# Starting two token blocks in halves: a new order for the first stage of a scan and two expert layers

## The chip, the cores and the metric

One core of a Trainium2 chip runs the whole program. The metric is the device time of one execution in microseconds (us). Engines are called PE (TensorE), DVE (VectorE), ACT (ScalarE), POOL (GpSimd) and SP (SyncE, which here only issues transfers); each takes its own instructions in the order in which they were written into its queue.

## The reference

Three layers, one after the other, for 3072 tokens of width 256 (4 sequences of 768 tokens, 8 heads of width 32).

```python
# 1. a scan over chunks of each sequence (state N=16 x D=32 for each head)
L = np.exp(cum[:, :, :, None] - cum[:, :, None, :]) * causal
M = np.einsum('bhin,bhjn->bhij', Cc, Bc) * L
y_intra = np.einsum('bhij,bhjd->bhid', M, xc)
y_inter = np.einsum('bhin,bhnd->bhid', Cc, state) * np.exp(cum)[:, :, :, None]
state = decay_full[:, :, None, None] * state + np.sum(Bx, axis=2)
# 2. a dense layer, 256 -> 2048 -> 256
h = x @ w_in
g = np.maximum(0.01 * h, h)
x = g @ w_out
# 3. each token goes to one of 8 experts, 256 -> 1024 -> 256
out[mask] = gate_w[mask, None] * (np.maximum(x[mask] @ w1[e], 0.0) @ w2[e])
```

`cum` is the running sum of log(a) within a chunk. `w_in` and `w_out` arrive as 8-byte floats.

## The kernel before

The 3072 tokens are 24 **chunks** of 128 (six to a sequence) and 6 **blocks** of 512 (four chunks each). A chunk c of the scan passes through named steps: `load` (tiles `ct`, `bt`, `xt`, and for chunks from 4 on `e`), `trmm`, `trc`, `trb`, `trd`, `trde` (transposes on PE and their evictions), `exp` (the decays L into `e`), `cb` and `mul` (the scores and their product with `e`), `bs`, `p3` (PE: output and state update), `st` (DVE: the state), `xa`, `xb` (the output as a high part `xh` by ACT and a rest `xl` by DVE). Each dense product runs as three products of such high and low parts.

The decays of chunks 0 to 3 are made on the chip (`bc`, into PSUM, then `exp`); their causal mask is a POOL instruction after `exp` (L445). For later chunks the running sums go out to DRAM (`cumd`, L364) and come back broadcast to all partitions as `e` (L394); POOL masks them (L399, before `exp`).

A block j of the dense layer has 16 **inner tiles** f of 128 columns. For one inner tile, written here with one number 16j+f: `h` is six matmuls of 512 columns on PE (L655), `sa` on ACT, `gg` on DVE, `gh` on ACT, `gl` on DVE, and `y` is six more matmuls (L695) that add into two PSUM banks which stay open over all 16 inner tiles. The two banks that hold `h` alternate, so `h` of one tile waits until `gg` of the tile two before it is done. `h.0` needs all four chunks of block 0, and from f=4 on each four inner tiles need another piece of the weights.

The weights come in four pieces of 1 MiB for each matrix (`raw.i.k`, `raw.o.k`) through three buffers, and each half piece is converted by two ACT steps (`hb`, `lb`), two DVE instructions (`or`, L605 and L606), one ACT cast and one subtraction on DVE or POOL.

What stands in which order is one long string, `PLAN`. Its tokens are run one by one, and on PE, DVE, ACT, POOL and SP the instructions keep that order. Ahead of it, outside of the string, stand the first loads, the constants (`consts_a`, `consts_b`) and nine matmuls on zeros that keep PE busy (L1107). Within the string, `warm` (L1127) and `wy` (L1133) are more matmuls on zeros. The third layer (`m1`, `m2`) follows when its tokens are sorted, from about 360 us on.

Of the kernel before, what the change touches and what calls it, by code (L numbers as in the profile page):

```python
# [19 lines left out]
NEG = -1.0e30  # L20
# [11 lines left out]
    bc.3.0 mul.1.2 trde.2 trc.2 p3.1 load.5 or.o.0.1 raw.i.2 trb.2 exp.3.0 exp.3.1 cb.2 bs.2 xa.1 st.1 cast.o.0.1
    trmm.3 xb.1 mask.3.0 trb.3 mul.2.1 cast.o.0.0 mask.3.1 mul.2.2 trc.3 subg.o.0.0 mul.2.3 mul.2.0 subv.o.0.1 wy.5.1
    p3.2 load.6 hb.i.1.0 cd.3 bs.3 cd.4 lb.i.1.0 cb.3 st.2 xa.2 or.i.1.0 trd.3 wy.3.2 hb.i.1.1 trde.3 lb.i.1.1 mul.3.3
    trmm.4 mul.3.0 trd.4 cast.i.1.0 mul.3.1 xb.2 trde.4 subg.i.1.0 mul.3.2 trb.4 trc.4 wy.3.3 p3.3 load.7 or.i.1.1
    raw.o.2 xa.3 xb.3 cast.i.1.1 st.3 wy.3.4 h.0 subv.i.1.1 mask.4 h.1 sa.0 cd.5 exp.4.0 gg.0 h.2 gh.0 mask.5 sa.1
    exp.4.1 gg.1 gl.0 h.3 gh.1 bs.4 mask.6 hb.o.1.0 y.0 lb.o.1.0 gl.1 hb.o.1.1 or.o.1.0 lb.o.1.1 y.1 sa.2 or.o.1.1
    raw.i.3 sa.3 cb.4 cast.o.1.0 exp.5.1 gg.2 subg.o.1.0 mul.4.1 h.4 mul.4.3 gh.2 mask.7 mul.4.2 hb.i.2.0 gg.3
    lb.i.2.0 mul.4.0 h.5 gl.2 cast.o.1.1 or.i.2.0 gh.3 trmm.5 sa.4 y.2 sa.5 subv.o.1.1 cast.i.2.0 gl.3 hb.i.2.1 trd.5
    p3.4 load.8 gg.4 subg.i.2.0 lb.i.2.1 gg.5 gh.4 y.3 or.i.2.1 raw.o.3 trb.5 hb.o.2.0 lb.o.2.0 h.6 gl.4 gh.5 or.o.2.0  # L40
    trde.5 exp.5.0 h.7 cd.7 st.4 sa.6 y.4 bs.5 sa.7 gl.5 cast.o.2.0 gg.6 xa.4 y.5 subg.o.2.0 gg.7 gh.6 xb.4 cast.i.2.1
    trc.5 exp.6.0 subv.i.2.1 cb.5 gl.6 h.8 hb.o.2.1 mul.5.1 mul.5.3 hb.i.3.0 mul.5.0 lb.o.2.1 y.6 mul.5.2 gh.7
    or.o.2.1 sa.8 h.9 lb.i.3.0 gg.8 cast.o.2.1 or.i.3.0 h.10 gh.8 sa.9 subv.o.2.1 exp.6.1 p3.5 gl.7 hb.i.3.1 gg.9
    trmm.6 load.9 y.7 lb.i.3.1 gl.8 trb.6 cast.i.3.0 or.i.3.1 h.11 sa.10 gh.9 gg.10 subg.i.3.0 cast.i.3.1 y.8 trc.6
    xa.5 subv.i.3.1 sa.11 mask.8 xb.5 hb.o.3.0 h.12 gh.10 gl.9 lb.o.3.0 gg.11 y.9 exp.7.0 bs.6 gl.10 cb.6 or.o.3.0
    exp.7.1 h.13 hb.o.3.1 mul.6.0 mul.6.2 cast.o.3.0 mul.6.1 y.10 mul.6.3 lb.o.3.1 subg.o.3.0 gh.11 p3.6 sa.12 bs.7
    gl.11 sa.13 trmm.7 gg.12 xa.6 load.10 trd.7 trb.7 y.11 trde.7 trc.7 gh.12 xb.6 st.6 exp.8.1 gl.12 h.14 gg.13
    exp.8.0 or.o.3.1 cb.7 sa.14 y.12 mul.7.1 gh.13 mul.7.2 mul.7.0 cast.o.3.1 h.15 mul.7.3 mask.9 gg.14 subv.o.3.1
    gh.14 trmm.8 gl.13 p3.7 sa.15 exp.9.0 gl.14 y.13 load.11 cd.8 gg.15 xa.7 trb.8 trc.8 exp.9.1 trd.8 xb.7 y.14 bs.8
    cd.9 bt trde.8 gh.15 h.16 gl.15 h.17 sa.16 bs.9 st.7 gg.16 cb.8 sa.17 gh.16 y.15 gg.17 mul.8.3 mul.8.2 h.18  # L50
    mul.8.1 evA.0 evV.0 gh.17 mul.8.0 mask.10 h.19 sa.18 gl.16 exp.10.1 lg.0 gg.18 p3.8 sa.19 lt.0 gl.17 exp.10.0
    cd.10 l2.0 load.12 st.8 trmm.9 trd.9 xa.8 h.20 r1.0 trde.9 trb.9 r2.0 rx.0 y.16 sa.20 xb.8 trc.9 gg.19 rp.0 gh.18
    r3.0 yr.0.0 be.0 y.17 yc.0.0 mask.11 gl.18 put.0 yr.0.1 exp.11.1 h.21 gg.20 gh.19 cd.11 bs.10 y.18 yc.0.1 gl.19
    sa.21 ro.0 exp.11.0 gg.21 trmm.10 trd.10 y.19 trc.10 trde.10 gh.20 trb.10 h.22 gl.20 gh.21 gl.21 h.23 sa.22 gg.22
    cb.9 sa.23 y.20 gg.23 mul.9.3 mul.9.2 y.21 mul.9.1 gh.22 mul.9.0 gl.22 p3.9 mask.12 gh.23 trmm.11 st.9 xa.9
    load.13 trd.11 trb.11 h.24 xb.9 trde.11 exp.12.1 trc.11 bs.11 gl.23 cb.10 sa.24 y.22 exp.12.0 mul.10.3 mul.10.1
    mul.10.2 mul.10.0 h.25 gg.24 gh.24 p3.10 sa.25 gl.24 gg.25 y.23 xa.10 load.14 st.10 xb.10 h.26 bs.12 gh.25 gl.25
    cb.11 sa.26 h.27 gg.26 mul.11.2 mul.11.1 y.24 mul.11.3 sa.27 mul.11.0 gg.27 p3.11 gh.26 gl.26 y.25 xa.11 load.15
    xb.11 h.28 gh.27 gl.27 y.26 sa.28 cd.13 gg.28 mask.13 y.27 gh.28 exp.13.1 gl.28 h.29 exp.13.0 h.30 sa.29 bs.13
    gg.29 y.28 sa.30 gh.29 gg.30 h.31 gl.29 gh.30 cd.14 gl.30 y.29 sa.31 mask.14 gg.31 trmm.12 exp.14.1 h.32 trc.12  # L60
    gh.31 y.30 trb.12 gl.31 sa.32 exp.14.0 gg.32 cb.12 y.31 gh.32 mul.12.3 mul.12.2 mul.12.0 mask.15 mul.12.1 h.33
    evA.1 evV.1 gl.32 exp.15.0 lg.1 sa.33 p3.12 lt.1 exp.15.1 gg.33 l2.1 st.12 load.16 trmm.13 r1.1 xa.12 h.34 trb.13
    gh.33 r2.1 rx.1 xb.12 y.32 sa.34 trc.13 r3.1 gg.34 rp.1 gl.33 h.35 gh.34 be.1 trd.13 sa.35 h.36 gl.34 put.1
    trde.13 gg.35 cb.13 bs.14 sa.36 cd.15 y.33 gg.36 mul.13.1 mul.13.0 h.37 mul.13.2 gh.35 mul.13.3 gl.35 p3.13 sa.37
    gg.37 yr.1.1 xa.13 load.17 st.13 y.34 yc.1.1 xb.13 bs.15 yr.1.0 gh.36 h.38 yc.1.0 gl.36 ro.1 y.35 sa.38 gg.38
    trmm.14 gh.37 trd.14 trc.14 h.39 trde.14 gl.37 trb.14 cd.16 mask.16 cb.14 sa.39 y.36 gg.39 exp.16.1 mul.14.2
    mul.14.3 h.40 mul.14.0 gh.38 mul.14.1 exp.16.0 gl.38 p3.14 sa.40 y.37 st.14 xa.14 load.18 xb.14 gg.40 y.38 gh.39
    bs.16 gl.39 trmm.15 gh.40 trd.15 trc.15 h.41 trb.15 gl.40 trde.15 cb.15 sa.41 h.42 gg.41 mask.17 mul.15.3 mul.15.2
    y.39 mul.15.0 sa.42 mul.15.1 exp.17.0 gg.42 p3.15 cd.17 gh.41 exp.17.1 y.40 gl.41 load.19 st.15 xa.15 bs.17 h.43
    gh.42 xb.15 gl.42 h.44 sa.43 gg.43 y.41 sa.44 gg.44 y.42 gh.43 gl.43 h.45 gh.44 gl.44 y.43 mask.18 sa.45 gg.45  # L70
    exp.18.1 h.46 gh.45 h.47 sa.46 gl.45 exp.18.0 gg.46 y.44 sa.47 y.45 gg.47 gh.46 gl.46 trmm.16 gh.47 h.48 trc.16
    trb.16 gl.47 trd.16 sa.48 y.46 mask.19 trde.16 gg.48 cb.16 gh.48 exp.19.1 h.49 mul.16.3 mul.16.1 mul.16.0 exp.19.0
    gl.48 y.47 mul.16.2 sa.49 p3.16 evV.2 evA.2 gg.49 lg.2 xa.16 load.20 st.16 gh.49 xb.16 h.50 lt.2 gl.49 bs.18 l2.2
    sa.50 trmm.17 r1.2 trd.17 trb.17 h.51 trde.17 r2.2 rx.2 trc.17 rp.2 sa.51 r3.2 trmm.18 be.2 y.48 trb.18 trc.18
    put.2 gg.51 cb.17 gg.50 y.49 mul.17.2 gh.50 mul.17.3 mul.17.0 h.52 gh.51 mul.17.1 gl.50 gl.51 p3.17 sa.52 cd.19
    gg.52 yr.2.1 xa.17 load.21 bs.19 y.50 yc.2.1 xb.17 h.53 gh.52 gl.52 cb.18 sa.53 y.51 gg.53 mul.18.2 mul.18.1 h.54
    mul.18.3 gh.53 mul.18.0 mask.20 yr.2.0 sa.54 gl.53 p3.18 yc.2.0 gg.54 exp.20.0 ro.2 trmm.19 load.22 st.18 y.52
    trc.19 cd.20 xa.18 trb.19 xb.18 exp.20.1 h.55 gh.54 bs.20 trd.19 y.53 sa.55 gl.54 trde.19 gg.55 h.56 gh.55 gl.55
    cb.19 sa.56 y.54 gg.56 mul.19.3 mul.19.1 h.57 mul.19.0 gh.56 mul.19.2 gl.56 p3.19 cd.21 sa.57 mask.21 gg.57 h.58
    xa.19 load.23 st.19 exp.21.0 xb.19 y.55 sa.58 exp.21.1 gg.58 y.56 gh.57 bs.21 h.59 gl.57 gh.58 gl.58 h.60 sa.59  # L80
    gg.59 mask.22 y.57 sa.60 gg.60 exp.22.0 y.58 gh.59 h.61 gh.60 gl.59 exp.22.1 gl.60 h.62 sa.61 gg.61 y.59 sa.62
# [1174 lines left out]
```

## Time and profile before

| | |
|---|---|
| median of 3 executions | 515.06 us (513.83 to 516.0) |
| the profiled execution | 515.77 us, of which the span from first to last instruction is 514.1 us |
| busy in the span | PE 495.4 us, DVE 327.0, ACT 288.1, POOL 138.1 |
| granted TensorE clock, mean | 0.993 of full speed |

The profiled execution is 0.7 us above the median. Outside of the span lie 1.7 us. Everything below is counted in the span of the profiled execution, from its first instruction.

### The profile page before, as it was taken

How to read it: one execution, taken by the hardware profiler on the slowest of the kernel's cores; microseconds unless marked ns; L12 is line 12 of the kernel's file. 1: busy time of each engine (PE TensorE's matmuls, PEld its weight loads, DVE VectorE, ACT ScalarE, POOL GpSimd, SP SyncE). 2: the span in 40 equal slices, each digit the busy share in tenths (PEclk: the TensorE clock that was granted, in tenths of full speed). 3: DMA queues.
4: the chain of work that ended last, by engine and by line, in shares of the span. 5: the costliest groups of instructions: out<-in, count | busy, mean ns of one | idle time of the engine just before them, and what ended most of it. 6: DMA issues, size and time to landing. Idle time of an engine off the chain costs nothing.

```text
span 514.1 us, 8931 instructions
## 1 busy us (share of the span) xinstructions
PE 495.4 (96%) x3266; PEld 393.5 (77%) x3266; DVE 327.0 (64%) x719; ACT 288.1 (56%) x626; POOL 138.1 (27%) x137
## 2 busy tenths in 40 slices
PE   7878999999999999999999999999999999999994
...
PEclk8999999999999999999999999999999999999998
DMA  7988863367713550417100661220015954310001
GB/s 153 195 190 210 231 162 68 62 89 26 156 20 63 103 112 7 68 15 169 35 1 2 172 232 52 37 8 0 2 42 115 325 177 166 117 52 32 11 21 68
DMA packets 120151, 48.41 MB, mean 94 GB/s; under 512 B 84066, under 2 KB 113891, under 8 KB 120099
## 3 DMA queue, kind: packets, MB, share of 16 engines
...
q0 software_dynamic: 3072, 6.41, 3.9%
...
## 4 chain that ended last, share of the span: by engine, by line
PE 72%; issue 8%; ACT 6%; DVE 5%; POOL 2%; DMA 2%; SPq 2%; POOLq 1%; ACTq 0%; DVEq 0%
PE y L695 22%; PE h L655 22%; PE hp L1025 10%; PE o L1056 9%; PE cb L512 2%; PE psy L552 2%; POOL out_dram L1086 1%; SPq L392 1%; DVE hb L606 1%; PE psy L547 1%; DMA ct<-in_C_dram 1%; PE xps L1006 1%; PE yr L852 1%; DMA e<-cumd 1%; DVE hb L605 1%
## 5 line engine op out<-in xcount | busy, mean ns | idle before, releaser
L662 ACT ACTIVATE sa<-h 128x512 f32<-128x512 f32 x96 | 56.9, 597 | 72.1 <-PE h L655 68.1
L667 DVE TENSOR_TENSOR gg<-sa,h 128x512 f32<-128x512 f32 x96 | 65.4, 685 | 48.4 <-ACT sa L662 47.2
L677 DVE TENSOR_TENSOR gl<-gg,gh 128x512 fp32r<-128x512 f32 x96 | 71.2, 748 | 15.4 <-ACT gh L672 14.0
L655 PE MATMUL h<-xh,wih 128*128 128x512 f32 x192 | 78.4, 408 | 1.0 <-DVE gg L667 1.0
L695 PE MATMUL y<-gh,woh 128*128 128x512 f32 x192 | 79.2, 412 | 0.0
L655 PE MATMUL h<-xl,wih 128*128 128x512 f32 x192 | 75.1, 391 | 0.9 <-DVE xl L576 0.9
L695 PE MATMUL y<-gl,woh 128*128 128x512 f32 x192 | 75.5, 393 | 0.3 <-DVE gl L677 0.3
L695 PE MATMUL y<-gh,wol 128*128 128x512 f32 x192 | 75.0, 391 | 0.0
L655 PE MATMUL h<-xh,wil 128*128 128x512 f32 x192 | 75.0, 391 | 0.0
L672 ACT CAST gh<-gg 128x512 fp32r<-128x512 f32 x96 | 59.1, 619 | 25.2 <-DVE gg L667 19.9
L1043 DVE SCALAR_TENSOR_TENSOR hl<-hp,hh 128x512 fp32r<-128x512 f32 x48 | 32.9, 689 | 59.0 <-ACT hh L1039 50.8
L1056 PE MATMUL o<-w2s,hh 128*128 128x256 f32 x384 | 70.1, 282 | 0.0
L1025 PE MATMUL hp<-x2h,w1s 128*128 128x512 f32 x192 | 65.8, 395 | 0.4 <-issue 0.3
L1039 ACT ACTIVATE hh<-hp 128x512 fp32r<-128x512 f32 x48 | 28.6, 598 | 61.2 <-PE hp L1025 53.9
L1056 PEld LDWEIGHTS o<-w2s,hh 128*128 128x128 f32 x384 | 61.1, 190 | 2.3 <-issue 0.2
L1056 PE MATMUL o<-w2s,hl 128*128 128x256 f32 x192 | 54.1, 282 | 0.0
L835 POOL DMA_INDIRECT il<-ids,pi x24 | 24.8, 1035 | 105.4 <-DVE base L826 67.9
L417 ACT ACTIVATE e<-e,ncum 128x128 f32<-128x128 f32 x160 | 50.5, 394 | 0.0
L399 POOL TENSOR_SCALAR_AFFINE_SELECT e<-e 128x1024 f32<-128x1024 f32 x20 | 23.9, 1195 | 92.1 <-DMA e<-cumd 68.7
L655 PEld LDWEIGHTS h<-xh,wih 128*128 128x128 f32 x192 | 36.0, 188 | 12.6 <-DVE gg L667 2.9
L695 PEld LDWEIGHTS y<-gh,woh 128*128 128x128 f32 x192 | 36.1, 188 | 11.7 <-issue 4.7
L1025 PEld LDWEIGHTS hp<-x2h,w1s 128*128 128x128 f32 x192 | 36.1, 188 | 8.3 <-issue 0.9
...
## 6 DMA issues: line engine op xcount, KB each, us to landing
...
```

The source lines that it names most:

```text
L417: s.activation(out=e[:, h, :], in_=i, func=AF.Exp, bias=ncum[:, cc, b * H + h:b * H + h + 1])
L655: t_.matmul(h, lhsT=w[:, k, fs], rhs=xx[:, k, :], start=(i == 0), stop=(i == 5))
L662: s.activation(out=d["sa"], in_=d["h"], func=AF.Copy, scale=0.01)
L667: v.tensor_tensor(out=d["gg"], in0=d["sa"], in1=d["h"], op=ALU.max)
L672: s.copy(out=d["gh"], in_=d["gg"])
L677: v.tensor_tensor(out=gl, in0=d["gg"], in1=d["gh"].bitcast(F32), op=ALU.subtract)
L695: t_.matmul(y_t[j][k], lhsT=w[:, f, ds], rhs=gg, start=(f == 0 and i == 0), stop=(f == NF - 1 and i == 2))
L835: w = g.indirect_dma_start(out=il[:], out_offset=IndirectOffsetOnAxis(ap=pi[:, q:q + 1], axis=0), in_=ids[:, c0 + q:c0 + q + 1], in_offset ...
L1025: t_.matmul(d["hp", f], lhsT=d[1][:, k, part, fs], rhs=xx[:, k, :], start=(n == 0), stop=(n == 5))
L1039: s.activation(out=e_h(i, f, "hh"), in_=ex[i]["hp", f], func=AF.Relu)
L1043: v.scalar_tensor_tensor(out=e_h(i, f, "hl"), in0=d["hp", f], scalar=0.0, in1=d["hh", f].bitcast(F32), op0=ALU.max, op1=ALU.subtract)
L1056: t_.matmul(d["o", q], lhsT=d[h, f][:, q * P:(q + 1) * P], rhs=d[2][:, f, part, :], start=(start and n == 0), stop=(f == NF2 - 1 and n == ...
```

## The change

Six things change together.

1. **Halves.** Blocks 0 and 1 run their inner tiles in the order block 0 tiles 0 to 7, block 1 tiles 0 to 7, block 0 tiles 8 to 15, block 1 tiles 8 to 15. After the first half of a block its two PSUM banks are copied to SBUF (`part_a` on ACT, `part_v` on DVE); after its second half two DVE additions put the halves together (`evict_a`, `evict_v`; before, one ACT copy and one DVE copy).
2. **Mask by TensorE.** For chunks 0 to 3 a matmul of an identity with a table of 0 and -1e30 opens each `bc` bank; the POOL masks of these chunks are gone.
3. **Decays from 96 rows.** `a` is loaded as 96 rows of 256 in place of 32 rows of 768; clip and logarithm run on that, and two transposes take the place of six.
4. **Loads in written order.** All loads and constants are tokens of the string now. `load` no longer contains the broadcast of `e`, which is a token of its own (`le`), as is the store of `cumd`.
5. **Fewer matmuls on zeros.** 6 in place of 9 at the start, none in place of 15 by `warm`, 8 in place of 14 by `wy`.
6. **A new order** of the whole string.

```diff
-    decay_a bc.0.0 decay_b cd.1 rows exp.0.0 hb.i.0.0 mask.0.0 bc.0.1 end high lb.i.0.0 cr trmm.0 hb.i.0.1 or.i.0.0
...
+    load.0 kg1 load.1 decay_a load.2 kvb kg2 kvc bc.0.1 raw.i.0 decay_b kg3 kv2 load.3 bc.0.0 exp.0.1 raw.o.0 trmm.0
...
+    HALF = NF // 2
...
-    a_sb = ap_.tile([NB * H, S], F32, tag="as", name="a_sb", bufs=1)
+    a_sb = ap_.tile([96, 2 * P], F32, tag="a96", name="a_sb", bufs=1)
...
+        g.affine_select(out=mkf, in_=mkf, pattern=[[1, P]], compare_op=ALU.is_ge, fill=NEG, base=0, channel_multiplier=-1)
+        v.tensor_copy(id16, ident)
+        v.tensor_copy(mk16, mkf)
...
-        for c in range(NCB):
-            t_.transpose(p0[:, c * BH:(c + 1) * BH], a_sb[:, c * P:(c + 1) * P], ident[:BH, :BH])
-        v.tensor_copy(laT.rearrange("p c r -> p (c r)"), p0[:, 0:NCB * BH])
+        for u in range(2):
+            t_.transpose(p0[:, u * 96:(u + 1) * 96], a_sb[:, u * P:(u + 1) * P], ident[:96, :96])
...
+    def attn_load_e(c):
+        b, cc = divmod(c, NCB)
+        sl = slice(cc * P, (cc + 1) * P)
+        e = ch[c]["e"] = e_tile(c)
+        nc.sync.dma_start(out=e, in_=cumd[b * H:(b + 1) * H, sl].unsqueeze(0).to_broadcast([P, H, P]))
...
+        t_.matmul(bc, lhsT=id16, rhs=mk16.unsqueeze(1).to_broadcast([P, 4, P]), start=True, stop=False)
...
-        if j not in y_t:
+        if (f == 0 and j not in y_t) or (f == HALF and j < 2):
             new_y(j)
+        first = (0, HALF) if j < 2 else (0,)
+        last = (HALF - 1, NF - 1) if j < 2 else (NF - 1,)
...
+    def part_a(j):
+        s.copy(out=yt_tile(j)[:, 0, :], in_=y_t[j][0])
...
     def evict_a(j):
-        s.copy(out=yt_tile(j)[:, 0, :], in_=y_t[j][0])
+        if j < 2:
+            v.tensor_tensor(out=yt_tile(j)[:, 0, :], in0=y_t[j][0], in1=yt_tile(j)[:, 0, :], op=ALU.add)
+        else:
+            s.copy(out=yt_tile(j)[:, 0, :], in_=y_t[j][0])
...
-    for _ in range(9):
+    for _ in range(6):
         t_.matmul(wps, lhsT=wt[:, 0:P], rhs=wt, start=True, stop=True)
```

Two places of the new order matter below. The first is SP's queue behind the constants' loads. Before, from the store of the running sums on (`e_402` and `e_496` are the broadcasts for chunks 4 and 5):

```order
L364 DMA cumd_96<-cumrow_264 32x768
L633 DMA raw_324<-in_moe_w_out_dram 128x4x256
L390 DMA ct_401<-in_C_dram 128x8x16
L391 DMA bt_400<-in_B_dram 128x8x16
L392 DMA xt_399<-in_x_dram 128x8x32
L394 DMA e_402<-cumd_96 128x8x128
L390 DMA ct_495<-in_C_dram 128x8x16
L391 DMA bt_494<-in_B_dram 128x8x16
L392 DMA xt_493<-in_x_dram 128x8x32
L394 DMA e_496<-cumd_96 128x8x128
```

Of the change, the same stretch of SP's queue (`e_400` and `e_514` are the broadcasts for chunks 4 and 5):

```order
L390 DMA cumd_96<-cumrow_277 32x768
L415 DMA ct_376<-in_C_dram 128x8x16
L416 DMA bt_375<-in_B_dram 128x8x16
L417 DMA xt_374<-in_x_dram 128x8x32
L431 DMA e_400<-cumd_96 128x8x128
L663 DMA raw_428<-in_moe_w_out_dram 128x4x256
L415 DMA ct_487<-in_C_dram 128x8x16
L416 DMA bt_486<-in_B_dram 128x8x16
L417 DMA xt_485<-in_x_dram 128x8x32
L431 DMA e_514<-cumd_96 128x8x128
```

The second piece of `w_out` moved from ahead of chunk 4 to behind it; ahead of chunk 5 the same transfers stand as before. The piece of `w_in` that followed `e_496` before now follows chunk 7.

The second place is ACT's queue around the first inner tiles. Before, the `exp` of chunk 4 (`e_402`) stands behind the first `sa` (`xh_152` is `xa` of chunks 2 and 3):

```order
L570 CAST xh_152<-psy_547 128x2x128
L595 ACTIVATE hb_596<-raw_208 128x512
L495 ACTIVATE cdt_599<-ps_523,mask2_106 128x128 x2
L600 ACTIVATE lb_597<-raw_208 128x512
L1148 CAST wih_137<-hb_569 128x512
L492 COPY cdt_612<-ps_604 128x128
L471 COPY btt_616<-ps_604 128x128
L570 CAST xh_152<-psy_623 128x2x128
L1148 CAST wih_137<-hb_596 128x512
L662 ACTIVATE sa_676<-h_658 128x512
L417 ACTIVATE e_402<-e_402,ncum_122 128x128 x4
```

Of the change, ACT's queue from the evictions of chunk 3's transposes on (`xh_156<-psy_525` is `xa` of chunk 2, `xh_156<-psy_590` that of chunk 3):

```order
L525 ACTIVATE cdt_522<-ps_506,mask2_106 128x128 x2
L453 ACTIVATE e_400<-e_400,ncum_125 128x128 x4
L600 CAST xh_156<-psy_525 128x2x128
L453 ACTIVATE e_400<-e_400,ncum_125 128x128 x4
L501 COPY btt_582<-ps_547 128x128
L630 ACTIVATE lb_503<-raw_266 128x512
L1176 CAST woh_146<-hb_472 128x512
L600 CAST xh_156<-psy_590 128x2x128
```

Both halves of chunk 4's `exp` moved ahead of `xa` of chunks 2 and 3, on which `h.0` depends. Of the change again, ACT's queue a few rows on (`xh_171` is `xa` of chunk 4, `sa_713` the first `sa`):

```order
L630 ACTIVATE lb_642<-raw_275 128x512
L453 ACTIVATE e_514<-e_514,ncum_125 128x128 x8
L600 CAST xh_171<-psy_685 128x2x128
L692 ACTIVATE sa_713<-h_628 128x512
L522 COPY cdt_716<-ps_676 128x128
L501 COPY btt_721<-ps_676 128x128
L692 ACTIVATE sa_723<-h_661 128x512
```

The `exp` of chunk 5 moved ahead of the first `sa`, too. On PE, `h.0` is followed by `cb` of chunk 4, `h.1`, the transposes of chunk 5, `p3` of chunk 4, `cb` of chunk 5 and then `h.2`; before, `h.0` to `h.3` and the first two `y` ran ahead of `cb` of chunk 4.

## Rows read from the trace of the kernel before

**Rows 1.** The page: PE's busy tenths in 40 slices, granted clock, DMA share.

```profile
PE   7878999999999999999999999999999999999994
PEclk8999999999999999999999999999999999999998
DMA  7988863367713550417100661220015954310001
```

**Rows 2.** Busy time by stretch: PE, PEld, DVE, ACT, POOL, PEclk, DMA share, GB/s.

```profile
0.00:37.91 37.91, 29.77 (x274) 17.29 (x274) 28.79 (x76) 24.56 (x56) 16.60 (x35) 0.95 0.85 179
39.30:70.50 31.20, 29.34 (x154) 21.25 (x154) 27.31 (x52) 28.09 (x65) 7.68 (x6) 1.00 0.85 219
70.50:130.00 59.50, 59.34 (x440) 44.58 (x439) 50.78 (x120) 44.15 (x115) 13.42 (x11) 1.00 0.52 66
130.00:362.00 232.00, 231.62 (x1452) 179.91 (x1451) 154.43 (x357) 128.13 (x286) 41.23 (x36) 1.00 0.33 69
```

**Rows 3.** Timeline of PE: start, length, line, tiles, count, idle before it.

```profile
1.27 3.87 PE L1107 MATMUL wps<-zer 128*128 128x512 bf16 x9 [1.27 <-DVE zer L1104]
29.68 0.67 PE L539 MATMUL psy<-cdt,st 128*128 128x256 f32 x2 [0.57 <-DVE xl L576]
37.91 0.50 PE L655 MATMUL h<-xh,wih 128*128 128x512 f32 x1
39.31 0.50 PE L655 MATMUL h<-xl,wih 128*128 128x512 f32 x1 [0.89 <-DVE xl L576]
45.79 0.39 PE L695 MATMUL y<-gh,woh 128*128 128x512 f32 x1
...
48.28 0.39 PE L695 MATMUL y<-gh,wol 128*128 128x512 f32 x1
48.60 0.71 PE L512 MATMUL cb<-cm,btt 32*128 32x256 f32 x8
54.50 0.27 PE L477 MATMUL ps<-ident,cd 128*128 128x128 f32 x1
55.80 0.49 PE L695 MATMUL y<-gh,woh 128*128 128x512 f32 x1
```

**Rows 4.** 39.3 to 70.5 us, instructions of L655 (h) alone, then of L695 (y).

```profile
39.30:70.50 31.20, 16.64 (x65) 11.66 (x65) 1.00 0.85 219
...
39.30:70.50 31.20, 11.11 (x42) 7.65 (x42) 1.00 0.85 219
```

**Rows 5.** SP's queue: issues, their length.

```profile
5.05 4.80 SPq L392 DMA_DIRECT2D xt<-in_x_dram  x1
25.15 0.37 SPq L633 DMA_DIRECT2D raw<-in_moe_w_out_dram  x1
30.54 0.53 SPq L394 DMA_DIRECT2D e<-cumd  x1
35.78 0.57 SPq L394 DMA_DIRECT2D e<-cumd  x1
```

**Rows 6.** Stretches of 10 us, as in rows 2.

```profile
20.00:30.00 10.00, 7.72 (x101) 4.81 (x99) 8.34 (x21) 7.98 (x20) 5.28 (x8) 1.00 0.92 233
30.00:40.00 10.00, 6.97 (x77) 3.81 (x76) 9.70 (x24) 4.97 (x12) 3.48 (x3) 1.00 0.82 164
50.00:60.00 10.00, 10.00 (x66) 7.49 (x66) 9.44 (x17) 8.61 (x20) 4.25 (x4) 1.00 0.93 275
```

**Rows 7.** Timeline of POOL, DVE and ACT.

```profile
41.27 1.09 POOL L399 TENSOR_SCALAR_AFFINE_SELECT e<-e 128x1024 f32<-128x1024 f32 x1 [2.90 <-DMA e<-cumd]
43.55 0.69 DVE L667 TENSOR_TENSOR gg<-sa,h 128x512 f32<-128x512 f32 x1 [1.48 <-ACT sa L662]
37.49 0.37 ACT L570 CAST xh<-psy 128x256 fp32r<-128x256 f32 x1 [1.63 <-PE psy L555]
40.76 0.60 ACT L662 ACTIVATE sa<-h 128x512 f32<-128x512 f32 x1 [1.19 <-PE h L655]
41.25 1.27 ACT L417 ACTIVATE e<-e,ncum 128x128 f32<-128x128 f32 x4
```

298 lines of the change are left out of this document (148 added, 150 removed).

## The prediction

> **What bounds the kernel now.** I read the page's slices first: PE is at nine tenths or more in every slice but the first four and the last, and it is at full clock from the second slice on [rows 1]. So PE's own work sets the time once it has begun, and only the first stage can give anything back. The stretches say where that stage ends: from 70.5 us on PE is busy 59.34 of 59.5 us and then 231.62 of 232 us, so nothing is left to gain there unless its work shrinks, and the change takes no matmul away behind that point [rows 2]. From 39.3 to 70.5 us PE is busy 29.34 of 31.2 us, but busy overstates it. PE's timeline shows one matmul of 512 columns every 0.226 us (12 of `y`, the first at 45.79, the last at 48.28, so 11 steps), one `cb` 0.71 us, and `p3` with its transpose 1.3 us (54.50 to 55.80) [rows 3]. In that stretch stand 65 matmuls of `h` and 42 of `y` [rows 4]: 107 times 0.226 is 24.2 us. With `cb` of chunks 4 and 5, `p3` of chunk 4 and a pair of transposes (0.27 us, as the one at 54.50) it is 27.2 us, so 4.0 us of the 31.2 are waits. Ahead of it lies the start: `h.0` begins at 37.91 and stalls for `xl` until 39.31 [rows 3].
>
> What is behind those two numbers? DMA. From the second slice on it is at eight or nine tenths for 60 us [rows 1], 0.92 in the third ten us [rows 6], and SP's queue itself is held up: the load of one `xt` takes 4.80 us to issue [rows 5], because the transfers ahead of it have not drained. What comes late is therefore set by how many bytes stand ahead of it. The broadcast `e` of chunk 5 is issued at 35.78 [rows 5] and the POOL mask that needs it starts at 41.27, after 2.90 us of idling for that transfer [rows 7]: 5.5 us from issue to use.
>
> **The change part by part.** Clip and logarithm on 256 columns in place of 768, two transposes for six, and no POOL mask behind the `exp` of the first chunks shorten the head of the chain. Two chunks' conversions move behind `h.0`. All of that is worth time only up to the next thing that is late. That is `e` of chunk 4. ACT's queue now has the first half of chunk 4's `exp` ahead of `xa` of chunk 2, and ACT takes its queue in order, so behind it wait `xa` of chunks 2 and 3, `xb` on DVE, `p3` of chunk 3 and `h.0`.
>
> When does that `e` come? Before, it was issued at 30.54 [rows 5], so with 5.5 us it was usable at 36.0. In the new order the same transfers stand ahead of it but for one piece of `w_out`, 1.05 MB. At the rate of the stretch in which that piece ran, 233 GB/s, this is 4.5 us; at the fastest and slowest of the rows 3.8 and 6.4 us [rows 6]. So it is usable between 29.6 and 32.2; I take 31.5. ACT is there before: `p3` of chunk 2 ran at 29.68 before [rows 3], and with less ahead of it will not be later. From there: mask 1.1 us to 32.6, half an `exp` 1.27 to 33.9, `xa` 0.37 to 34.2 [rows 7]. Then `xb`, four products by DVE and `p3` of chunk 3 (some 2 and 1.3 us) bring `xa` of chunk 3 to 37.5, where it was before, at 37.49 [rows 7]. The second matmul of `h.0` comes at 39.3, as before. All that was saved at the head is waited away.
>
> The next late thing is `e` of chunk 5. Ahead of it stand the same transfers as before, so it is usable at 41.3. All of chunk 5's `exp` now stands ahead of `xa` of chunk 4 and the first `sa`: mask to 42.4, two halves of 1.27 to 44.9, `xa` to 45.3, `sa` 0.60 to 45.9, `gg` 0.69 to 46.6 [rows 7]. Only then may `h.2` take the first bank; `cb` of chunk 5, queued ahead of it, waits for ACT's evictions behind `sa` and ends at about 47.0. PE meanwhile has `h.0`, `cb` of chunk 4, `h.1`, the transposes and `p3` of chunk 4, from 39.3 to about 44.1, and then waits 2.3 us.
>
> From 47.0 the first half of block 0 needs 14 more inner products (`h.2` to `h.7`, `y.0` to `y.7`): 84 matmuls, 19.0 us; `p3` of chunks 5 to 7, 3.9; two `cb`, 1.4; two pairs of transposes, 0.5. That is 24.8 us, to 71.8. I add 0.7 for small waits, a sixth of the 4.0 found above, because ACT and DVE have half of the conversions left to do by then: 72.5.
>
> The kernel before has at 70.5 us `h.0` to `h.10` and `y.0` to `y.6`, two products more (2.7 us), but lacks the 5.8 us of chunks 5 to 7. It reaches the same amount of work at 73.6. The change is 1.1 us ahead. The new turns between halves cost something: at the end of each half PE goes on with `h` of the other block while ACT and DVE copy the banks, so the cover is some 5 us of matmuls against a copy of about 0.6 us; uncovered, four turns would cost 2.4. The two additions on DVE in place of a copy each on ACT and DVE lie beside PE's work, too. I take 0.5 us. The 24 matmuls on zeros that go, and the eight mask matmuls that come, lie in the stage that waits for DMA and are put at nothing; the first as cover for the clock come up below.
>
> Sum: 515.77 - 1.1 + 0.5 = 515.2 us against the profiled execution, and that was 0.7 above the median of the three runs: **514.5 us**.
>
> **A rule against it.** The kernel before spends 38 matmuls on zeros at the start and shows a mean granted clock of 0.95 up to 37.91 us and 1.00 after that [rows 2]. The nine first ones run at 0.43 us each, which is the lower level, 1.2 GHz, against 0.226 at 2.4 GHz [rows 3]. In the change 14 are left, and PE has almost nothing to do while ACT waits for chunk 4's `e`. The Trainium skill, page "TensorE: Matmul & The Clock Gate", section "HAM oscillation — how this bites in real kernels", tells of a kernel whose PE waited for DMA between bursts of matmuls and began each burst at the halved clock. By that rule `h.0`, `h.1`, `cb` and `p3` would start at 1.2 GHz and the sum would be 516 to 517 instead of 515.2; no stretch of the trace of before shows such a wait ahead of `h`, so it can't settle it.
>
> **The rivals.**
> *The transfers come sooner.* SP is never held up by the order it had before, small transfers run together, and the rate rises. For it: 275 GB/s in one stretch [rows 6]. Against: DMA at 0.92 and 0.93 already [rows 6], with the same packets. Each us by which chunk 5's `e` is sooner is a us of the result. From 2 us on (usable at 39.2) it is faster than the bound; at 4 us, 511.
>
> *The clock falls.* Between `p3` of chunk 2 (by about 30) and `p3` of chunk 3 (about 36) PE has little more than a `cb`, a pair of transposes and four matmuls on zeros, so some 4 us of waiting. At half clock `h.0` and `h.1` take 2.4 us longer (12 times 0.2) and `cb` and `p3` up to 2.0, of which the 2.3 us of waiting absorb half: 1 to 2 us. That alone leaves it within the bound. It decides if the lower level holds beyond 47 us, where PE is the bound again: every 2 us cost 1, so from about 50 us on it is slower; held for 10 us, 519.
>
> *DVE becomes the bound.* From 39.3 to 70.5 DVE is busy 27.31 us and ACT 28.09 of 31.2 [rows 2]. The change packs chunks 5 to 7 into the 25 us from 47 on; 16 `gg` and `gl` at 0.69 us [rows 7] are 11 us of DVE's time there, and with three chunks and four or five conversions I estimate it at 23 to 25 us. If it can't run ahead of PE, 3 to 4 us go: 518. For the other side, half of the conversions are due only later.
>
> **How the numbers follow.** A measurement of this kernel can tell about 0.5%, 2.6 us, from no change. My forecast, a change that does at its head what it says and waits it away at chunks 4 and 5, has a chance of 0.52 and lies within that bound, from 512.5 to 517.5. The sooner transfers have 0.25 (faster, around 511), the clock that stays low 0.14 and DVE 0.09 (both slower, 518 to 519). The range reaches into both sides: 510.3 to 519. Faster 0.25, same 0.52, slower 0.23.
>
> **What would show it.** In the profile after: the `exp` of chunk 4 ends several us of idle time on ACT, released by the mask or by `e`, at about 32.6 us; the first matmul of `h` with `xl` at 39.3 (between 38 and 40); `exp` of chunk 5 at 42.4 and the first `sa` at 45.3; a gap on PE ahead of `cb` of chunk 5 of 2.3 us; the first `h` of block 1 at 72.5; after that PE busy without gaps. I am wrong if `h` begins before 36, if the clock in the stretch from 40 to 50 us is well under 1, or if PE waits for `gg` or `gl` between 47 and 72 us by more than 2 us, or at the turns between the halves by more than 1.

## The result, and the profile after

The changed kernel takes 517.40 us (median of 20 runs, 514.35 to 520.07), the kernel before 514.92 (20 runs beside it): a ratio of 1.0052, interval 1.0033 to 1.0071. It is slower by half a per cent. The time lies inside the range and, by 0.1 us, inside the bounds given for the likeliest case (512.5 to 517.5); but that case had the kernel unchanged, at 514.5, and against the kernel beside it, it is slower.

The first stage by windows of ten us: busy us of each engine with counts, granted TensorE clock (1.00 is 2.4 GHz, 0.50 is 1.2 GHz), DMA's share and rate.

```profile
30.00:40.00 10.00, 5.25 (x35) 2.50 (x33) 5.25 (x13) 5.06 (x15) 2.96 (x3) 0.53 0.94 214
40.00:50.00 10.00, 8.15 (x68) 5.59 (x68) 9.39 (x24) 8.54 (x22) 3.71 (x4) 1.00 0.94 232
70.00:80.00 10.00, 10.00 (x66) 8.03 (x59) 9.37 (x16) 8.24 (x18) 2.85 (x2) 1.00 0.84 208
80.00:90.00 10.00, 9.19 (x40) 7.00 (x38) 9.83 (x17) 8.55 (x21) 4.29 (x3) 1.00 0.08 31
90.00:100.00 10.00, 9.37 (x42) 7.72 (x42) 9.83 (x16) 9.07 (x19) 1.30 (x1) 1.00 0.01 2
```

Two things differ from the windows of before [rows 2, 6]. From 30 to 40 us PE is busy for only 5.25 us of ten, and for most of that time at the lower clock. And from 80 to 100 us PE is idle for 1.44 us, where before it was busy for 59.34 of 59.5 us; DVE stands at 9.83 of 10 there.

ACT in the first stage (start, length, line, what it writes and reads, and in brackets the idle time ahead and what ended it):

```profile
33.08 1.28 ACT L453 ACTIVATE e<-e,ncum 128x128 f32<-128x128 f32 x4 [5.84 <-POOL e L435]
34.27 0.35 ACT L600 CAST xh<-psy 128x256 fp32r<-128x256 f32 x1
38.31 0.37 ACT L600 CAST xh<-psy 128x256 fp32r<-128x256 f32 x1 [1.29 <-PE psy L585]
42.75 2.44 ACT L453 ACTIVATE e<-e,ncum 128x128 f32<-128x128 f32 x8
45.77 0.60 ACT L692 ACTIVATE sa<-h 128x512 f32<-128x512 f32 x1
```

These are `exp` of chunk 4, `xa` of chunks 2 and 3, `exp` of chunk 5 and the first `sa`. ACT stands still for 5.84 us until chunk 4's mask is done; the forecast had these rows at 32.6, 34.2 (the end of a half), 37.5, 42.4 and 45.3. PE's rows that answer to them, and those of the new waits:

```profile
35.81 1.19 PE L569 MATMUL psy<-cdt,st 128*128 128x256 f32 x2 [4.75 <-DVE xl L606]
40.44 0.50 PE L685 MATMUL h<-xl,wih 128*128 128x512 f32 x1 [0.29 <-DVE xl L606]
47.95 0.50 PE L685 MATMUL h<-xh,wih 128*128 128x512 f32 x1 [0.18 <-DVE gg L697]
73.41 0.39 PE L685 MATMUL h<-xh,wih 128*128 128x512 f32 x1
87.26 0.50 PE L727 MATMUL y<-gl,woh 128*128 128x512 f32 x1 [0.81 <-DVE gl L707]
90.70 0.50 PE L685 MATMUL h<-xh,wih 128*128 128x512 f32 x1 [0.63 <-DVE gg L697]
94.91 0.39 PE L685 MATMUL h<-xh,wih 128*128 128x512 f32 x1
```

The second matmul of `h.0` comes at 40.44 (before 39.31 [rows 3]), `h.2` at 47.95, and `h.16`, the first of block 1, at 73.41. Nothing is wrong up to there that would cost 2.5 us. The two waits at 87.26 and 90.70 are new.

A later point shows where this leaves the change. When `y.29` starts, both kernels have exactly the same `h`, `y`, `cb` and `p3` behind them. PE's row there, of the change and of the kernel before:

```profile
149.05 0.50 PE L727 MATMUL y<-gh,woh 128*128 128x512 f32 x1
147.22 0.39 PE L695 MATMUL y<-gh,woh 128*128 128x512 f32 x1
```

The change is 1.83 us late there. DVE just ahead of the two waits and in the first stage, and then POOL:

```profile
37.82 1.65 DVE L636 SCALAR_TENSOR_TENSOR hb<-raw,hb 128x512 int32<-128x512 int32 x1
39.97 0.42 DVE L606 TENSOR_TENSOR xl<-psy,xh 128x256 fp32r<-128x256 f32 x1
79.83 0.69 DVE L635 SCALAR_TENSOR_TENSOR hb<-hb,lb 128x512 int32<-128x512 int32 x1
81.16 0.68 DVE L697 TENSOR_TENSOR gg<-sa,h 128x512 f32<-128x512 f32 x1
82.41 1.81 DVE L635 SCALAR_TENSOR_TENSOR hb<-hb,lb 128x512 int32<-128x512 int32 x1
84.25 1.46 DVE L636 SCALAR_TENSOR_TENSOR hb<-raw,hb 128x512 int32<-128x512 int32 x1
85.63 1.57 DVE L707 TENSOR_TENSOR gl<-gg,gh 128x512 fp32r<-128x512 f32 x1
```

```profile
37.10 1.81 POOL L1178 TENSOR_TENSOR wol<-hb,woh 128x512 fp32r<-128x512 f32 x1 [4.05 <-ACT woh L1176]
82.37 1.30 POOL L1178 TENSOR_TENSOR wol<-hb,woh 128x512 fp32r<-128x512 f32 x1 [6.84 <-ACT woh L1176]
83.61 3.04 POOL L435 TENSOR_SCALAR_AFFINE_SELECT e<-e 128x1024 f32<-128x1024 f32 x2
```

The conversion (`or`, L635 and L636) and `gl` take 0.69 us on DVE when POOL is idle, and 1.46 to 1.81 us from 82.41 to 87.2, while POOL subtracts and masks chunks 10 and 11 (82.37 to 86.65). The `gl` that PE waits for at 87.26 is one of them.

### The profile page after: what moved, and what is told of

It reads as the page before. It is cut to its first block, busy times and chain, and to the rows that moved or that the text cites. A ratio compares the mean times of both kernels' runs of the same rounds, so it can differ in the third digit from the quotient of the medians.

```text
span 514.9 us, 8880 instructions
## 1 busy us (share of the span) xinstructions
PE 494.5 (96%) x3245; PEld 394.6 (77%) x3246; DVE 334.0 (65%) x725; ACT 288.4 (56%) x626; POOL 132.4 (26%) x131
## 4 chain that ended last, share of the span: by engine, by line
PE 80%; issue 7%; DVE 7%; POOL 2%; ACT 2%; DMA 1%; POOLq 0%; SPq 0%; DVEq 0%; ACTq 0%
PE y L727 25%; PE h L685 24%; PE hp L1061 9%; PE o L1092 9%; PE cb L542 3%; PE psy L582 2%; POOL out_dram L1122 2%; DVE e L550 1%; PE psy L577 1%; DVE hb L635 1%; PE yr L888 1%; DVE hb L636 1%; PE xps L1042 1%; DMA e<-cumd 1%; DVE gg L697 1%
## 5 line engine op out<-in xcount | busy, mean ns | idle before, releaser
L707 DVE TENSOR_TENSOR gl<-gg,gh 128x512 fp32r<-128x512 f32 x96 | 68.9, 721 | 14.9 <-ACT gh L702 13.5
L727 PEld LDWEIGHTS y<-gl,woh 128*128 128x128 f32 x192 | 36.1, 188 | 8.4 <-DVE gl L707 2.2
L685 PEld LDWEIGHTS h<-xh,wil 128*128 128x128 f32 x192 | 36.1, 188 | 7.9
```

Source lines behind the costliest of these rows:

```text
L685: t_.matmul(h, lhsT=w[:, k, fs], rhs=xx[:, k, :], start=(i == 0), stop=(i == 5))
L707: v.tensor_tensor(out=gl, in0=d["gg"], in1=d["gh"].bitcast(F32), op=ALU.subtract)
L727: t_.matmul(y_t[j][k], lhsT=w[:, f, ds], rhs=gg, start=(f in first and i == 0), stop=(f in last and i == 2))
```

## The experiments

Theories. *Queue*: the head's gain is waited away on ACT behind `e` of chunks 4 and 5. *Clock*: PE's idling costs the upper clock, and that costs time. *DVE*: what is new is the stretch at 80 to 100 us, where DVE can't keep up, by itself or because POOL holds it up. All edits but three (head_only, halves_only, and in before_few0 the number of zeros at the start) are in the order string; `h.16` and `h.8` (the first of block 0's second half) are read in each run's one trace.

| kernel | median us (runs) | ratio to the kernel before beside it | h.16 | h.8 | between |
|---|---|---|---|---|---|
| the change | 517.40 (20) | 1.0052 (1.0033 to 1.0071) | 73.4 | 94.9 | 21.5 |
| after_again | 517.59 (9) | 1.0043 (1.0028 to 1.0058) | 74.3 | 95.8 | 21.5 |
| zeros | 518.06 (12) | 1.0045 (1.0022 to 1.0069) | 76.2 | 97.7 | 21.5 |
| zeros28 | 516.94 (12) | 1.0052 (1.0031 to 1.0073) | 72.8 | 94.2 | 21.5 |
| q4 | 516.72 (12) | 1.0020 (0.9999 to 1.0041) | 73.4 | 94.9 | 21.5 |
| q45 | 518.94 (6) | 1.0092 (1.0071 to 1.0113) | 78.0 | 99.5 | 21.5 |
| q45b | 514.96 (12) | 1.0003 (0.9983 to 1.0024) | 72.2 | 93.7 | 21.5 |
| subg | 516.87 (7) | 1.0061 (1.0039 to 1.0083) | 73.7 | 95.2 | 21.5 |
| late80 | 514.95 (12) | 1.0006 (0.9987 to 1.0025) | 73.8 | 93.2 | 19.5 |
| q45b_late | 513.37 (12) | 0.9973 (0.9955 to 0.9990) | 71.1 | 90.6 | 19.5 |
| masks_late | 519.69 (12) | 0.9942 (0.9913 to 0.9971), see below | 73.9 | 93.8 | 19.8 |
| bt_late | 518.64 (12) | 0.9940 (0.9910 to 0.9970), see below | 74.3 | 94.8 | 20.6 |
| halves_only | 517.62 (12) | 1.0043 (1.0017 to 1.0068) | 75.9 | 97.4 | 21.5 |
| head_only | 520.57 (6) | 1.0093 (1.0057 to 1.0129) | | | |
| before_few0 | 515.41 (12) | 1.0024 (1.0010 to 1.0037) | | | |

**The clock.** Kernel zeros adds 16 matmuls on zeros, zeros28 adds 30, into PE's wait for chunk 4:

```diff
-p3.2 bs.3 exp.4.0 or.o.0.0 trmm.4 load.6 cb.3 xa.2 st.2 exp.4.1 wy.4.1
+p3.2 wy.6.0 bs.3 exp.4.0 or.o.0.0 trmm.4 load.6 cb.3 xa.2 st.2 exp.4.1 wy.14.1
```

> The changed kernel with 16 more matmuls on zeros on PE: six behind p3 of chunk 2 and ten more (14 in place of 4) behind cb of chunk 3, where PE has nothing else to do. Theory 'clock': the granted clock of 0.53 in 30 to 40 us comes from PE's idling, so it rises to near 1 there, p3 of chunk 3 takes 1.3 us again in place of 2.4, the second matmul of h.0 comes at 39.3 to 39.6 in place of 40.44, and the kernel gains 0.8 to 1.4 us on the change. Rival 'queue': what is late is xa on ACT behind exp of chunk 4, so h.0 stays behind 39.3 whatever the clock and the time moves by less than 0.8 us. If the zeros run at the lower level themselves, the clock can't be had back here and nothing moves.

It did not test the theory: PE still waited 4.12 us after its zeros and fell to the lower clock. In its trace the clock also fell a second time, behind `h.2` (granted 0.84 from 50 to 60 us), and there `h.2` to `h.16` took 26.5 us in place of the change's 25.5. So, with `wy.28.1` in place of `wy.14.1`, and the change itself beside it:

> As zeros, but 28 matmuls on zeros behind cb of chunk 3 in place of 14, so that PE is busy from 29.6 to about 36 us, to just ahead of the moment at which p3 of chunk 3 can run in the change (35.81). Theory 'clock': the granted clock stays at 1.00 from 20 to 50 us, p3 of chunk 3 takes 1.3 us in place of 2.4, and the second matmul of h.0, exp of chunk 5, h.2 and h.16 each come about 1 us sooner behind the mask of chunk 4 than in the change (there 7.4, 9.7, 14.9 and 40.4 us behind its end at 33.05); 0.8 to 1.2 us less than the change beside it. Rival 'queue alone': these distances stay as they are, or h.0 is later because the zeros stand ahead of it.

> The changed kernel itself, beside zeros28 on one chip, since the two differ by an us at most. Every theory expects the distances from the end of the mask of chunk 4 as in its first trace, and h.16 between 73 and 76 with that mask's end between 33 and 34.5.

Windows, PE and DVE of zeros28:

```profile
30.00:40.00 10.00, 8.32 (x58) 3.98 (x56) 5.61 (x14) 5.35 (x16) 2.90 (x2) 1.00 0.88 202
```

```profile
36.34 0.63 PE L582 MATMUL psy<-e,xt 128*32 128x128 f32 x14 [0.23 <-DVE e L550]
40.08 0.50 PE L685 MATMUL h<-xl,wih 128*128 128x512 f32 x1 [1.53 <-DVE xl L606]
37.45 1.65 DVE L636 SCALAR_TENSOR_TENSOR hb<-raw,hb 128x512 int32<-128x512 int32 x1
39.61 0.42 DVE L606 TENSOR_TENSOR xl<-psy,xh 128x256 fp32r<-128x256 f32 x1
```

The clock is 1.00 and `p3` of chunk 3 takes 1.7 us in place of 2.4 (from 35.44 to its last transpose at 37.12; in the change from 35.81 to 38.16), yet `h.0` waits 1.53 us for `xl`: its second matmul stands 7.39 us behind the end of chunk 4's mask (32.69), as in the change (33.05). `h.16` is 40.1 us behind it against 40.4. In after_again the two distances are 7.93 and 40.7 us (its mask ends at 33.63), half a microsecond more than in the change's first trace, though it is the same kernel. So of the 0.8 to 1.2 us that the clock theory asks, the traces show between none and 0.6, and the times, alike within their intervals, can't tell so little. The theory does not explain the 2.5 us: what was late is `xl` on DVE, behind a conversion that took 1.65 us beside POOL's subtraction. Most or all of what the fallen clock costs hid in that wait.

In the kernel before the zeros are worth something. before_few0 has the change's number of them (9 to 6 on `wps`, no `warm`, `wy` 14 to 8):

> The kernel before with the change's number of matmuls on zeros: 6 in place of 9 at the start, none in place of 15 on the bank of chunk 1, 8 in place of 14 (two at each of the four places). Theory 'the zeros kept the clock': the granted clock falls to about 0.5 to 0.85 for a part of 10 to 45 us and the kernel loses 1 to 2.5 us: 516 to 517.5. Rival 'the stage waits for DMA anyway': the clock may fall, but p3 and h.0 come at the same times, 514.5 to 515.3.

```profile
20.00:30.00 10.00, 8.82 (x101) 5.60 (x99) 7.95 (x19) 8.46 (x21) 4.86 (x7) 0.80 0.87 208
30.00:40.00 10.00, 7.39 (x70) 3.93 (x71) 9.77 (x24) 4.75 (x13) 4.11 (x4) 0.83 0.86 183
```

The clock falls to 0.80 and 0.83, `h.0` starts at 38.9 in place of 37.9, and the kernel is 1.1 us slower than the one before beside it (514.27).

**The queue.** q4 moves `exp` of chunk 4 behind `xa` of chunk 3:

```diff
-p3.2 bs.3 exp.4.0 or.o.0.0 trmm.4 load.6 cb.3 xa.2 st.2 exp.4.1
+p3.2 bs.3 or.o.0.0 trmm.4 load.6 cb.3 xa.2 st.2
...
-p3.3 or.o.0.1 trd.4 xa.3 load.7
+p3.3 or.o.0.1 trd.4 xa.3 exp.4.0 exp.4.1 load.7
```

> The changed kernel with one move on ACT's queue: both halves of exp of chunk 4 behind xa of chunk 3 in place of ahead of xa of chunk 2. PE's, DVE's and SP's orders stay. Theory 'queue': ACT no longer idles 5.84 us for e of chunk 4; xa of chunk 2 runs at about 28 in place of 34.27, p3 of chunk 3 at about 31, the second matmul of h.0 at 34 to 35.5 in place of 40.44, and since PE is the bound from there on the kernel is 2 to 5 us faster than the change (512 to 515). Rival 'something later is the bound': weights' conversions on DVE and ACT are next; h.0 is as early as said, but PE then waits for gg, gl or weights before 100 us and the time is within 1 us of the change.

ACT and PE of q4:

```profile
27.35 0.37 ACT L600 CAST xh<-psy 128x256 fp32r<-128x256 f32 x1
33.12 2.45 ACT L453 ACTIVATE e<-e,ncum 128x128 f32<-128x128 f32 x8 [1.46 <-POOL e L435]
41.92 2.44 ACT L453 ACTIVATE e<-e,ncum 128x128 f32<-128x128 f32 x8 [3.68 <-POOL e L435]
33.62 0.50 PE L685 MATMUL h<-xl,wih 128*128 128x512 f32 x1 [1.06 <-DVE xl L606]
47.17 0.80 PE L685 MATMUL h<-xh,wih 128*128 128x512 f32 x1 [0.46 <-DVE gg L697]
```

`h.0` is 6.8 us sooner, and not one of them is left: ACT now waits 3.68 us for chunk 5, `h.2` comes at 47.17, at the lower clock (granted 0.66 from 40 to 50 us), and `h.16` at 73.4 as before the edit. The first wait was real, the second one takes its place: the rival had it right.

q45 clears the second as well, ACT and DVE doing `sa`, `gg` and conversions ahead of chunk 5's `exp` and products, and `y.0` ahead of `p3` of chunk 5:

```diff
-h.1 mul.4.0 exp.5.1 mul.4.3 mul.4.1 mul.4.2 trmm.5 or.i.1.0 exp.5.0 p3.4
+sa.0 hb.i.1.0 cd.5 h.1 mul.4.0 mul.4.3 mul.4.1 mul.4.2 trmm.5 gg.0 hb.i.1.1 gh.0 lb.i.1.0 p3.4 or.i.1.0
...
+cast.i.1.0 gl.0 gh.1 h.2 subg.i.1.0 or.i.1.1 sa.2 exp.5.1 exp.5.0
```

> The changed kernel with ACT's and DVE's queues written so that nothing stands behind e of chunk 4 or 5 that doesn't need it: exp of chunk 4 behind xa of chunk 3, exp of chunk 5 behind xa of chunk 4, sa of h.0 to h.2 and the conversion of the second piece of w_in; gg, gl and that conversion ahead of bs and the products of chunk 5 on DVE; y.0 ahead of p3 of chunk 5 on PE. Theory 'queue, twice': in q4 the 6.8 us won at h.0 were waited away at exp of chunk 5, and h.4 waited for its weights (converted on DVE by 53.9 us). Here h.2 comes at 40 to 42 in place of 47.2, h.4 at 46 to 49 in place of 54.1, h.16 at 68 to 71 in place of 73.4, and since all later times follow h.16 the kernel is 2.5 to 5 us faster than the change: 512.5 to 515. Rival 'DMA': e of chunks 6 and 7 (usable at about 46 and 51) and the pieces of w_in and w_out come at the same times as before and take the gain: h.16 at 72.5 or later, time within 1 us of the change.

It was badly written, and 1.5 us slower than the change by the medians, 2.1 to 2.5 by the ratios: `trc` of chunk 5 stood on DVE behind a conversion that waited for ACT, and `cb` of chunk 5, ahead of `h.2` on PE, waited 3.97 us for that chain. q45b unties it:

```diff
-h.1 mul.4.0 mul.4.3 mul.4.1 mul.4.2 trmm.5 gg.0 hb.i.1.1 gh.0 lb.i.1.0 p3.4 or.i.1.0 trd.5 mask.6 trc.5 trb.5 xa.4
+h.1 mul.4.0 mul.4.3 mul.4.1 mul.4.2 trmm.5 trb.5 gg.0 trc.5 hb.i.1.1 lb.i.1.0 gh.0 p3.4 trd.5 mask.6 xa.4
...
+h.2 sa.1 xb.4 trde.5 st.4 gl.0 cb.5 le.8 gg.1 sa.2 or.i.1.0
```

> q45 written again without the knot found there (trc of chunk 5 stood on DVE behind a conversion that waited for ACT, and btt, cb of chunk 5 and h.2 behind that; exp of chunk 5 stood behind sa of h.2). Order now: sa.0, gg.0, trc and xb of chunk 5 and 4 ahead of the conversion; h.2 ahead of cb of chunk 5; y.0 and y.1 ahead of p3 of chunk 5; exp of chunk 5 behind sa.2. Theory 'queue, twice': h.2 at 39 to 41 in place of 48.0, h.4 at 47 to 50 in place of 54.1, h.16 at 68 to 71.5 in place of 73.4; 512.5 to 515.5. Rival 'DMA': the order no longer matters once e of chunks 6 and 7 come late; h.16 at 72.5 to 74 and 516.5 to 517.5.

PE of q45b:

```profile
40.62 0.48 PE L685 MATMUL h<-xh,wih 128*128 128x512 f32 x1
50.87 0.49 PE L577 MATMUL psy<-cdt,st 64*128 64x128 f32 x4 [2.44 <-DVE e L550]
72.22 0.39 PE L685 MATMUL h<-xh,wih 128*128 128x512 f32 x1
```

`h.2` is 7.3 us sooner than in the change, then 2.44 us go to the products of chunk 5, and `h.16` is 1.2 sooner in this trace, less than the 68 to 71.5 expected. The kernel is level with the one before, 2.1 to 2.5 us better than the change (0.0040 to 0.0049 of the ratio).

**80 to 100 us.** subg gives four subtractions of DVE's to POOL:

```diff
-subv.i.2.1
+subg.i.2.1
...
-subv.o.2.1
+subg.o.2.1
```

and the same for `i.3.1` and `o.3.1`.

> The changed kernel with the four subtractions of conversions that DVE does for pieces 2 and 3 of w_in and w_out (0.68 us each) on POOL in place of DVE (1.30 us each). Theory 'DVE is the bound at 80 to 100 us': the two waits of PE there (0.97 and 0.80 us, for gl and gg) shrink by 1 us or more and the kernel gains 1 to 2 us on the change: 515.5 to 516.5. Rival: what PE waits for is the order in which DVE does the conversion of piece 2 ahead of gl and gg, not the amount, and POOL's slower subtraction holds buffers longer: within 0.5 us of the change or slower.

PE, DVE and POOL of subg:

```profile
90.97 0.50 PE L685 MATMUL h<-xh,wih 128*128 128x512 f32 x1 [1.69 <-DVE gg L697]
88.39 1.01 DVE L327 TENSOR_SCALAR m<-m 128x24 f32<-128x24 f32 x1
87.23 2.14 POOL L435 TENSOR_SCALAR_AFFINE_SELECT e<-e 128x1024 f32<-128x1024 f32 x2
```

The time is the rival's, no better than the change: there is one wait of 1.69 us in place of two. POOL's masks now run beside the bias table, whose operation takes 1.01 us there and 0.18 in the change. Work moved from DVE to POOL came back as longer operations on DVE. late80 instead takes the masks and the table out of the stretch:

```diff
-subg.o.2.0 gg.20 trb.8 exp.8.0 subv.o.2.1 mask.10 y.19 bt sa.21 mask.11
+subg.o.2.0 gg.20 trb.8 exp.8.0 subv.o.2.1 y.19 sa.21
...
+sa.13 gl.12 gg.13 mask.10
...
+gl.15 bt
```

(`exp` of chunks 10 and 11 move behind them.)

> The changed kernel with work taken out of 80 to 100 us: the POOL masks of chunks 10 and 11 with their exp on ACT, and the six small operations of the bias table on DVE, come behind h.13 to h.15 (110 to 120 us, where DVE and ACT are half idle). In the change's trace the same DVE operations on two SBUF tiles take 0.69 us alone and 1.33 to 1.81 us while POOL runs its masks or subtractions; 82.4 to 87.1 us is such a stretch. Theory 'POOL slows DVE there': the waits of PE at 86 and 90 us (0.81 and 0.63 us by the trace) go, h.8 comes 1.2 to 1.8 us sooner after h.16 than the 21.5 us of the change, and the kernel gains as much: 515.6 to 516.3. Rival 'the sum of gg, gl and conversions is too much for DVE by itself': the waits only move to 95 to 105 us and the time stays within 0.5 us of the change.

PE and DVE of late80:

```profile
86.67 0.39 PE L727 MATMUL y<-gl,woh 128*128 128x512 f32 x1
89.17 0.39 PE L685 MATMUL h<-xh,wih 128*128 128x512 f32 x1
82.79 1.81 DVE L635 SCALAR_TENSOR_TENSOR hb<-hb,lb 128x512 int32<-128x512 int32 x1
84.63 0.69 DVE L636 SCALAR_TENSOR_TENSOR hb<-raw,hb 128x512 int32<-128x512 int32 x1
85.25 0.69 DVE L707 TENSOR_TENSOR gl<-gg,gh 128x512 fp32r<-128x512 f32 x1
```

Both waits are gone. The two operations that stood beside the masks are back at 0.69 us, the one beside POOL's subtraction still takes 1.81. `h.8` comes 19.5 us behind `h.16` in place of 21.5, `y.29` starts at 147.62, 0.40 us behind the kernel before, and the kernel is level with it, a little better than expected. Which half does it?

> Of late80 the one half: POOL's masks of chunks 10 and 11 and their exp behind h.13 to h.15, the bias table where the change has it. If POOL's masks are what slowed DVE: the conversion and gl behind them take 0.69 us each in place of 1.46 and 1.57, both waits of PE shrink and most of the 2.4 us of late80 comes, 515 to 516. If the bias table was the cause: as the change, 517 to 517.8.

> Of late80 the other half: the six operations of the bias table (1.43 us of DVE's time from 88.5 us on) behind h.15, the masks where the change has them. If the bias table alone was the cause, 515 to 516. If POOL's masks were: the wait for gl at 86 us stays, that for gg at 90 us goes (0.63 to 0.8 us), 516.3 to 517.

Beside these two the kernel before took 522.56 us, eight more than beside the others, so their times are not set against the rest, what was expected of them stays undecided, and only the stretch up to `h.8` is read. PE and DVE of masks_late, and PE of bt_late:

```profile
89.57 0.50 PE L685 MATMUL h<-xh,wih 128*128 128x512 f32 x1
84.79 0.69 DVE L636 SCALAR_TENSOR_TENSOR hb<-raw,hb 128x512 int32<-128x512 int32 x1
85.40 0.69 DVE L707 TENSOR_TENSOR gl<-gg,gh 128x512 fp32r<-128x512 f32 x1
```

```profile
88.09 0.50 PE L727 MATMUL y<-gl,woh 128*128 128x512 f32 x1 [0.78 <-DVE gl L707]
```

Without POOL's masks the wait for `gl` is gone and the other is too short to be listed (19.8 us between `h.16` and `h.8`); without the table the wait for `gl` stays at 0.78 and that for `gg` goes (20.6). Both count, the masks more.

**Together.** q45b_late has q45b's order and late80's:

> Both edits, q45b and late80. If both theories hold: 511 to 514, at or below the kernel before. If only one holds, the time of that one.

513.37 us, ratio 0.9973 (0.9955 to 0.9990): faster than the kernel before beside it, and by the ratios than the change. q45_subg has q45's order and subg's:

> Both edits, that of q45 and that of subg. If each theory holds they add: 3.5 to 6.5 us less than the change, 511 to 514, faster than the kernel before. If h.16 earlier only lengthens the waits at 80 to 100 us (conversions come when their transfers do), the gain of q45 is lost there and the two together are no better than q45 alone.

519.53 us (6 runs; ratio 1.0083, 1.0056 to 1.0110): `h.16` at 76.8 and again 21.5 us to `h.8`; neither edit gains.

**Head and halves apart.** head_only takes the change's order up to `h.2`, then that of the kernel before with whole blocks; halves_only the reverse, with the code of the kernel before and the halves added:

```diff
-        first = (0, HALF) if j < 2 else (0,)
-        last = (HALF - 1, NF - 1) if j < 2 else (NF - 1,)
+        first = (0,)
+        last = (NF - 1,)
```

> Blocks 0 and 1 whole, as before: the changed kernel's order up to h.2 (TensorE mask, decays from 96 rows, loads in written order, its few zeros), then the order of the kernel before. Theory 'the head gave nothing, the halves cost': h.0 at 39.6 to 40.5 as in the change, and 514 to 515.5, since only the late h.0 (1.1 us) stands against it. Theory 'the head itself costs': 516.5 to 518, like the change. If the halves are what pays in the change and the head costs, it is slower than the change.

> The head of the kernel before (its order up to h.2, its loads, its zeros, masks by POOL), then blocks 0 and 1 in halves in the order of the change. Theory 'halves cost' (PE waits at 80 to 100 us where DVE is at 0.98, turns between the halves, packed attention of chunks 8 to 11): 516.5 to 518. Theory 'head costs': 514 to 515.5, no slower than the kernel before, with h.0's second matmul at 39.3 and PE waits at 80 to 100 us below 1.

PE of head_only and of halves_only:

```profile
53.31 0.50 PE L685 MATMUL h<-xh,wih 128*128 128x512 f32 x1 [2.83 <-DVE gg L697]
```

```profile
89.76 0.50 PE L698 MATMUL y<-gl,woh 128*128 128x512 f32 x1 [0.79 <-DVE gl L678]
93.20 0.50 PE L656 MATMUL h<-xh,wih 128*128 128x512 f32 x1 [0.63 <-DVE gg L668]
```

head_only's 520.57 us lie outside of both of its expectations. Neither total is a price of its half, for each has a seam where two orders meet: in head_only PE waits 2.83 us there, and halves_only's `h.16` comes at 75.9. But the waits of 0.79 and 0.63 come with the halves' order alone, under the head and the zeros of the kernel before.

## Why the prediction was wrong

The sum was 515.2 us for the profiled execution, which took 516.65.

*The head is waited away at chunk 4.* Right. ACT's 5.84 us of idling end at 33.08, released by the mask, where its end was forecast for 32.6. `exp` of chunk 5 (42.75 for 42.4), the first `sa` (45.77 for 45.3) and `h.2` (47.95 for 47.0) follow the forecast at 0.4 to 1 us behind it; PE's wait ahead of `cb` of chunk 5 was 1.38 us, not 2.3, as `h.0` and `p3` ended later. q4 and q45b show that the wait is a matter of order and not of DMA alone.

*24.8 us of work and 0.7 of waits from `h.2` on.* Right: 25.46 us (47.95 to 73.41), forecast 25.5. DVE kept up, at the count of conversions expected.

*`xa` of chunk 3 at 37.5 and `h.0` at 39.3.* Mis-sized by 1.1 us. `xl` of chunk 3 stood behind a conversion of 1.65 us. This lateness runs on over `wol`, `hb` and `lb` to `exp` of chunk 5, whose mask had ended at 41.05. So it was by luck that `exp` of chunk 5 came near its forecast: `e` was there 1.3 us sooner than forecast (its mask starts at 39.96), and ACT was late for another reason. That chain is read from the trace; POOL's subtraction at 37.10 was not moved in a run.

*The turns cost 0.5 us, and after `h.16` PE is busy without gaps.* This is the step that failed. The turns cost nothing that the trace shows; the gaps came 13 and 17 us behind the first of them. From the point of equal work (73.6 before, `h.16` in the change, as the prediction's count has it) to the last matmul it is 433.3 us before (to 506.91) and 434.7 in the change (to 508.13): 1.4 us more in place of 0.5. PE's two waits show 0.81 and 0.63 us of idling, but they cost 2.0: `h.16` to `h.8` takes 21.5 us with them and 19.5 without (late80), and the matmul behind each wait starts 1.20 and 1.03 us behind the one ahead of it, where the step is 0.23 elsewhere. At `y.29` the change is 1.83 us behind the kernel before, late80 0.40. Of that, 0.6 us comes back behind the dense layer; no run shows why. The rival "DVE becomes the bound" had the engine right and the place wrong: I looked for it from 47 to 72 us, where chunks 5 to 7 are packed, and took the stage behind it from the trace of before, though the halves bring pieces 2 and 3 of the conversions, POOL's masks and 16 `gg` and `gl` together there. It also counted DVE's work at its length alone, not beside POOL.

*The transfers come sooner.* This did not decide: chunk 5's mask ended at 41.05, where 42.4 was forecast, but ACT was not free for it.

*The clock falls.* It did, to 0.53 from 30 to 40 us, and `p3` of chunk 3 ran at the lower level, as the rule of the Trainium skill, page "TensorE: Matmul & The Clock Gate", section "HAM oscillation — how this bites in real kernels", has it. `h.0`, `h.1` and `cb`, which were to begin there too, ran at 1.00 in this trace. In the time it counted for little here: it was back at 1.00 ahead of `h.2`, and zeros28 at 1.00 gains nothing that its times can tell.

The sum is therefore 0.9 us short ahead of `h.16` and 0.9 behind it; the last matmul to the end gives 0.4 back. The other 1.45 us between 514.5 and 517.40 lie in the sum's last step, from the profiled execution to the median: before's profiled one was 0.85 us above the median of its 20 runs, the change's 0.75 below, and I had assumed the same offset for both. The second trace of the change shows one place where executions part: chunk 4's mask ends at 33.63 in place of 33.05, `h.16` comes 0.9 us later, and from there to the last matmul it is 434.9 us against 434.7.

Left open: what spreads the executions of one kernel; why the kernel before took 522.56 us beside masks_late and bt_late; how much of the 1.1 us at `h.0` POOL's subtraction costs; and what the mask by TensorE and the 96 rows are worth by themselves, since no run has them alone.
